# FNet mixing with a GEGLU gate on one core: kept row tiles loaded one unit sooner, rows of g loaded through GpSimd's queue

## The chip, the cores and the metric

The kernel runs on one core of a Trainium2 chip, in float32. The time is that of the device in microseconds (us), the median of several runs. A core has five engines with a queue of instructions each: TensorE (PE, with its weight loads shown apart as PEld), VectorE (DVE), ScalarE (ACT), GpSimd (POOL) and SyncE (SP). SP and POOL also issue DMAs here: SP's are the profile's queue q1, POOL's are q0. All of them run on the core's 16 DMA engines.

## What is computed

x has S = 2048 rows of D = 448, and F = 1792. The reference, cut to what matters:

```python
xn = layernorm(x)
a, b = xn @ dft_hid_re.T, xn @ dft_hid_im.T          # hidden DFT
s = dft_seq_re @ a - dft_seq_im @ b                  # sequence DFT, real part
g = silu((gelu(xn @ w_gate) * (xn @ w_up)) @ w_down) # gate
out = x + s * g
```

## The kernel before, in words

Every matmul operand is split into a high and a low part, and a product is built from two or three matmuls of the parts. The rows are handled in 16 row tiles of 128 (NK = 16).

**The stages.** First the gate g is made (gate and up products, gelu, down product) and collected in SBUF. Then comes the hidden DFT, one row tile k at a time, while g goes through silu (line 930) and is stored row tile by row tile in a DRAM buffer gs (line 931, seen as gv). The hidden DFT leaves, for 14 of the 16 row tiles, an operand TS[k] of seven combinations, split into high and low parts; two row tiles (KP) are kept plain. The last stage, which the change touches, is the sequence DFT with the final product. It begins at about 491 us.

**The last stage.** The output rows are made in eight pairs j of row tiles t. A pair is 16 units u (the loop over `units`, lines 1023 to 1108; m counts units over all pairs). Units 0 to 13 each take one row tile k of TS and do seven products of Strassen's kind into seven PSUM banks (`seven`, lines 975 and 978: a 448-column matmul and a 224-column one for each product, in the order of PRODUCTS). Units 14 and 15 do the two plain row tiles (`plain`). A pair of u = 12 and 13 is done product by product in the last pair (line 1032).

**What is kept and what is reloaded.** Ten of the 14 operands stay in SBUF (KR). The other four (KX: row tiles 4, 5 and 0, 1) share two places, the tiles that the profile calls ts_u: two of them are used in units 0 and 1 of a pair, the other two in units 12 and 13, and the next pair begins with those. All four were saved to DRAM in the stage before (td, line 844, on POOL's queue). So in each pair the two places must be loaded anew between units 0 and 1, which read the old content, and units 12 and 13, which read the new. The load is cut in eight quarters of 392 KB, quarters 0 to 3 for the first place and 4 to 7 for the second (lines 1034 to 1042): quarter i is issued by SP in unit LOAD_AT + i, in the last pair in unit LOAD_AT + i * 7 // 8, which puts its first two in one unit. These loads are the profile's ts_u<-td. A quarter must wait until the matmuls that read what it overwrites are done.

**The left operands.** For each unit the slices of the sequence DFT come from DRAM: ct (192 KB) and sums (128 KB) for units 0 to 13, cp (256 KB) for units 14 and 15 (`load_c`, lines 875 to 882, into buffers that the profile calls raw, f or cc). `sum_c` forms two sums on VectorE (lines 888 and 889), and `prep_c` splits the result: ScalarE copies the high part (line 119), VectorE subtracts for the low part (line 120). `prep_c(m + 3)` is called in unit m, and when it has read its buffer it issues `load_c(m + 8)`. So SP's queue in unit m holds, in this order: the quarter of ts_u if there is one, a load of g if there is one, the loads for unit m + 8, and a store of the output if there is one.

**The end of a pair.** The seven banks are combined by VectorE in units 13 and 14 (`gather`, lines 998 to 1006). In units 0 to 4 of the next pair one step each follows (`give`, lines 1009 to 1019): an addition, in units 1 and 4 the multiplication by g (line 1013) and behind it a DMA on POOL's queue that adds x to the result (line 1015, cc<-x). The stores go out on SP's queue in units 5 and 8 (STORE_AT, line 1017, out<-cc).

**Rows of g.** `load_gx` (line 961) loads the two row tiles of g that pair j needs, 224 KB each, into the ends of two tiles (the profile's ts_g<-gs) in units 11 and 12 (GX_AT). They are read in units 1 and 4 of the next pair, or at the very end (line 1079) in the last one.

The order on each queue is the order of the program; the framework puts in the waits on semaphores that the data need.

Of the kernel before, what the change touches and what calls it, by code (L numbers as in the profile page):

```python
# [45 lines left out]
def fnet_geglu(ctx: ExitStack, tc: tile.TileContext, x, ca, ct, cp, et, wgu, wd, out):  # L46
# [13 lines left out]
    nc = tc.nc  # L60
# [360 lines left out]
    with tc.manual_schedule():  # L421
# [320 lines left out]
        gv = gs.rearrange("p (k d) -> p k d", k=NK)  # L742
# [3 lines left out]
        def place(tag, n):  # L746

            if tag not in new:
                new[tag] = sb.tile([P, n], FR, name=f"ts_{tag}", tag=tag)
            return new[tag]  # L750
# [200 lines left out]
        gx = [place(f"g{t}", 8 * D)[:, T7:].bitcast(F32) for t in range(2)]  # L951
# [6 lines left out]

        def load_gx(j, t):
            if 2 * j + t < NK:  # L960
                nc.sync.dma_start(gx[t], gv[:, 2 * j + t])


        LOAD_AT = 2
        STORE_AT = 5, 8
        GX_AT = 11, 12
        PRODUCTS = {1: (1, 0), 6: (3, 5), 2: (2, 2), 7: (5, 3), 5: (4, 4), 3: (6, 6), 4: (0, 1)}
# [55 lines left out]
        for m, (j, k) in enumerate(units):  # L1023
# [3 lines left out]
            if u < NS:  # L1027
# [7 lines left out]
                for i in range(8):  # L1035
                    if u != LOAD_AT + i * over // 8:
                        continue
# [8 lines left out]
            if u in GX_AT:  # L1046
                load_gx(j, GX_AT.index(u))
# [118 lines left out]
```

## Time and profile before

| | us |
|---|---|
| median of 3 runs | 786.28 (786.23 to 787.33) |
| the profiled execution | 785.82 |
| its span, first to last instruction | 783.9 |
| TensorE busy | 774.9 |
| VectorE busy | 593.7 |
| ScalarE busy | 308.9 |
| GpSimd busy | 51.8 |

The span is what the trace shows; the profiled execution's own time includes what lies around it. A row of a timeline gives the start, the duration, engine, line, operation, what it writes and reads, and in brackets the engine's idle time before it with what ended it. A row of waits gives who waited for what: us in total, times, longest. "To landing" is the time from a DMA's issue to its last byte's semaphore. A stretch view gives the length, the busy time of PE, PEld, DVE, ACT and POOL (with counts), the granted clock of TensorE, the busy share of the 16 DMA engines, and GB/s.

### The profile page before, as it was taken

The page shows a single profiled execution, that of the slowest core. Times are in us where ns is not written, and L with a number is a line of the kernel's source. Part 1 is how long each engine was busy: PE and PEld are TensorE (multiplying, and loading weights), DVE is VectorE, ACT ScalarE, POOL GpSimd, SP SyncE. Part 2 cuts the span into 40 slices and gives each one's busy share as a digit, 9 for nine tenths or more (in the row PEclk, how much of TensorE's full clock was granted, in tenths as well). Part 3 has the DMA queues.
Part 4 walks back from the last instruction along what each step waited for, and adds up shares of the span by engine and source line. Part 5 has one row for each costly group of instructions (what it writes and reads, how often), then busy time and mean ns, then how long its engine had stood idle before and what let it go on. Part 6 is the DMA issues. An engine that isn't in the chain of part 4 may idle for free.

```text
span 783.9 us, 11188 instructions
## 1 busy us (share of the span) xinstructions
PE 774.9 (99%) x4092; PEld 695.4 (89%) x4092; DVE 593.7 (76%) x1045; ACT 308.9 (39%) x430; POOL 51.8 (7%) x82
## 2 busy tenths in 40 slices
PE   9999999999999999999999999999999999999997
PEld 7888888888888888888889999999999999999996
DVE  7877876767766776776675676888888796969686
ACT  3874432331332322322232864544343444444341
POOL 1000211110110010100000000000000000000000
PEclk9999999999999999999999999999999999999999
DMA  8000575353292360546101651778796959697794
GB/s 319 25 3 25 167 220 117 121 121 117 48 258 55 121 135 10 161 131 158 34 13 52 254 229 51 239 256 277 245 318 212 350 172 367 198 322 231 279 278 166
DMA packets 62007, 134.37 MB, mean 171 GB/s; under 512 B 6784, under 2 KB 43520, under 8 KB 61056
## 3 DMA queue, kind: packets, MB, share of 16 engines
q1 hardware_dynamic: 56912, 109.22, 39.7%
q0 software_dynamic: 4896, 24.32, 14.2%
q8 instruction: 32, 0.52, 0.3%
q14 instruction: 23, 0.19, 0.1%
q10 hardware_dynamic: 144, 0.11, 0.0%
HBM read 119.87 MB, written 43.12 MB: 208 GB/s over the span
## 4 chain that ended last, share of the span: by engine, by line
PE 73%; DMA 12%; DVE 10%; issue 2%; SPq 1%; ACT 0%; DVEq 0%
PE x L346 23%; PE po L326 17%; PE ab L803 9%; PE p L975 8%; PE x L354 6%; PE p L978 4%; PE gu L276 4%; DMA ts_u<-td 3%; DMA out<-cc 3%; DVE xt L120 3%; DVE w L120 2%; DMA f<-sums 2%; DMA raw<-sums 2%; DMA raw<-ct 1%; DMA raw<-wgu 1%
## 5 line engine op out<-in xcount | busy, mean ns | idle before, releaser
L326 PE MATMUL po<-wd,hs 128*128 128x448 f32 x672 | 153.0, 366 | 0.0
L326 PEld LDWEIGHTS po<-wd,hs 128*128 128x128 f32 x672 | 125.7, 188 | 14.4
L346 PE MATMUL x<-xt,w 128*128 128x512 f32 x504 | 135.0, 391 | 0.0
L346 PEld LDWEIGHTS x<-xt,w 128*128 128x128 f32 x504 | 94.6, 188 | 16.9
L335 DVE TENSOR_TENSOR gacc<-gacc,po 128x448 f32<-128x448 f32 x96 | 59.1, 618 | 60.9 <-PE po L326 60.9
L119 ACT ACTIVATE w<-raw 128x896 fp32r<-128x896 f32 (+1 forms) x61 | 55.3, 908 | 72.6 <-DVE raw L889 33.7
L346 PE MATMUL x<-thl,w 128*128 128x512 f32 x288 | 77.5, 391 | 0.3 <-DVE tmp L406 0.3
L803 PE MATMUL ab<-w,xt 128*128 128x448 f32 x256 | 68.0, 365 | 0.0
L346 PEld LDWEIGHTS x<-thl,w 128*128 128x128 f32 x288 | 54.0, 188 | 11.6 <-DVE tmp L406 0.7
L354 PE MATMUL x<-xt,w 128*128 128x512 f32 x192 | 59.2, 390 | 0.0
L975 PE MATMUL p<-xt,w 128*128 128x448 f32 x168 | 54.1, 374 | 0.0
L401 ACT ACTIVATE hs<-tmp 128x512 fp32r<-128x512 f32 x24 | 15.2, 634 | 95.3 <-DVE tmp L399 95.3
L803 PEld LDWEIGHTS ab<-w,xt 128*128 128x128 f32 x256 | 48.1, 188 | 3.8
L386 ACT ACTIVATE tmp<-x 128x512 f32<-128x512 f32 x24 | 14.4, 599 | 89.4 <-PE x L354 89.4
L119 ACT ACTIVATE w<-f 128x896 fp32r<-128x896 f32 (+1 forms) x34 | 30.3, 891 | 48.0 <-DVE f L889 26.8
L120 DVE TENSOR_TENSOR w<-raw,w 128x896 fp32r<-128x896 f32 (+1 forms) x41 | 43.0, 1048 | 4.1 <-ACT w L119 3.6
L354 PEld LDWEIGHTS x<-xt,w 128*128 128x128 f32 x192 | 36.0, 188 | 7.7
L975 PE MATMUL p<-ts_u,w 128*128 128x448 f32 x112 | 37.3, 379 | 1.7 <-DMA ts_u<-td 0.7
L975 PE MATMUL p<-ts_u,ts_tmp 128*128 128x448 f32 x112 | 36.5, 374 | 0.0
L888 DVE TENSOR_TENSOR raw<-raw 128x128 f32<-128x128 f32 x69 | 19.9, 288 | 21.2 <-DMA raw<-sums 21.2
L975 PE MATMUL p<-hs,w 128*128 128x448 f32 x112 | 35.6, 374 | 0.0
L803 PE MATMUL ab<-wd,xt 128*128 128x448 f32 x96 | 35.1, 365 | 0.0
(234 smaller groups left out, 1600.0 us busy)
## 6 DMA issues: line engine op xcount, KB each, us to landing
ts_u<-td SPq DMA_DIRECT2D x64, 392.0 KB, 5.9
sums<-ca SPq DMA_DIRECT2D x16, 896.0 KB, 7.5
sums<-ca POOLq DMA_DIRECT2D x16, 896.0 KB, 9.5
raw<-ct SPq DMA_DIRECT2D x69, 192.0 KB, 4.5
raw<-sums SPq DMA_DIRECT2D x69, 128.0 KB, 4.5
f<-ct SPq DMA_DIRECT2D x39, 192.0 KB, 4.4
raw<-wgu SPq DMA_DIRECT2D x14, 512.0 KB, 4.2
td<-ts_u POOLq DMA_DIRECT2D x4, 1568.0 KB, 6.6
```

The lines of the kernel that those rows point to most:

```text
L119: nc.scalar.activation(h, src, AF.Copy)
L120: nc.vector.tensor_sub(l, src, h)
L276: nc.tensor.matmul(ps[:, cols], a, xt[:, k, cols], start=n == 0, stop=n == len(mm) - 1)
L326: nc.tensor.matmul(po[:, :D], hs[:, a, kk * P : (kk + 1) * P], wdn[:, b, i], start=n == 0, stop=n == 5,)
L335: nc.vector.tensor_add(ga, ga, po[:, :D])
L346: nc.tensor.matmul(ps, a[i], b[j], start=first and n == 0, stop=n == 2, skip_group_check=True)
L354: nc.tensor.matmul(ps, w["k3" + "gu"[g]][0], xt[:, 3], start=False, stop=True, skip_group_check=True)
L401: nc.scalar.activation(hs[:, 0], g1, AF.Copy)
L803: nc.tensor.matmul(p[:, :D], a, b, start=n == 0, stop=n == len(mm) - 1)
L888: nc.vector.tensor_add(s2, cr1, s1)
L975: nc.tensor.matmul(ps[q][:, :D], h, v, start=u % UN == 0, stop=False, skip_group_check=True)
L978: nc.tensor.matmul(ps[q][:, :HD], l, v[:, :HD], start=False, stop=u % UN == NS - 1, skip_group_check=True,)
```

## The change

Two edits. LOAD_AT goes from 2 to 1: each quarter of the kept row tiles is issued one unit sooner, in units 1 to 8 in place of 2 to 9 (in the last pair 1 to 7 in place of 2 to 8). And `load_gx` issues its DMA on GpSimd's queue in place of SP's; the place in the program stays (units 11 and 12), but POOL's queue holds nothing else of the stage than the two accumulating DMAs of line 1015.

```diff
         def load_gx(j, t):
             if 2 * j + t < NK:
-                nc.sync.dma_start(gx[t], gv[:, 2 * j + t])
+                nc.gpsimd.dma_start(gx[t], gv[:, 2 * j + t])
...
-        LOAD_AT = 2
+        LOAD_AT = 1
```

## The prediction

> **What bounds the kernel now.** First the page, for which engine sets the time.
>
> ```profile
> span 783.9 us, 11188 instructions
> PE 774.9 (99%) x4092; PEld 695.4 (89%) x4092; DVE 593.7 (76%) x1045; ACT 308.9 (39%) x430; POOL 51.8 (7%) x82
> ```
>
> TensorE is busy 774.9 of 783.9 us (its granted clock is 1.00 in the stretches shown below), and the edit touches none of its work. So the edit can only fill holes between matmuls, or make new ones. The next view is the waits of the weight loads (PEld) from 520 us on, pairs 1 to 7 of the last stage. I take weight loads, not matmuls, because they follow each other with hardly a gap, so that a wait stands there in full.
>
> ```profile
> PEld p L975 <- issue: 1.0, 2, 0.6
> PEld p L975 <- DMA ts_u<-td: 1.0, 2, 0.6
> PEld p L975 <- DMA f<-sums: 0.7, 1, 0.7
> PEld p L975 <- DMA raw<-sums: 0.6, 1, 0.6
> ```
>
> Those are six waits, 1.0 + 1.0 + 0.7 + 0.6 = 3.3 us, all at line 975: **that is all there is to win**. Now the timeline of TensorE around the hole of pair 6, with the start of that pair's unit 1 (708.76) and unit 8 (724.11) ahead of it.
>
> ```profile
> 708.76 0.37 PE L975 MATMUL p<-ts_u,w 128*128 128x448 f32 x1
> ...
> 724.11 0.38 PE L975 MATMUL p<-xt,ts_tmp 128*128 128x448 f32 x1
> ...
> 735.08 0.37 PE L975 MATMUL p<-ts_u,w 128*128 128x448 f32 x1
> 735.29 0.26 PE L978 MATMUL p<-ts_u,w 128*128 128x224 f32 x1
> 736.00 0.44 PE L975 MATMUL p<-ts_u,w 128*128 128x448 f32 x1 [0.45 <-DMA f<-sums]
> ```
>
> Seven units take 724.11 - 708.76 = 15.35 us, 2.19 us each. A matmul of 448 columns holds the stream for 0.21 us (735.08 to 735.29) and one of 224 half as long, so after the one at 735.29 the second product of unit 13 was due at 735.39; it began at 736.00. It reads columns of ts_u that the last two quarters of the second kept tile bring. Which transfer was late is seen in SP's timeline of that pair, and from its issue to landing for the last quarter alone (issued 730.15).
>
> ```profile
> 711.61 0.43 SPq L882 DMA_DIRECT2D f<-sums  x1
> ...
> 714.21 0.38 SPq L1042 DMA_DIRECT2D ts_u<-td  x1
> ...
> 729.35 0.34 SPq L1017 DMA_DIRECT2D out<-cc  x1
> 730.15 0.32 SPq L1042 DMA_DIRECT2D ts_u<-td  x1
> ...
> 734.02 0.32 SPq L961 DMA_DIRECT2D ts_g<-gs  x1
> ```
>
> ```profile
> DMA to landing us min/median/max: 5.7/5.7/5.7
> ```
>
> 730.15 + 5.7 = 735.85, 0.15 us ahead of the delayed matmul. The profile's label names f<-sums, but what the product reads came by the last ts_u quarter; I take it for the releaser of all six holes. Why it lands late shows in the stretch views, from the first quarter's issue to the last one's landing and in a quiet stretch after it (last two numbers: DMA share, GB/s).
>
> ```profile
> 714.21:735.86 21.65, 21.34 (x137) 20.11 (x135) 16.36 (x31) 9.20 (x11) 1.75 (x2) 1.00 1.02 341
> 738.00:750.30 12.30, 12.30 (x74) 11.60 (x73) 12.13 (x24) 4.79 (x5) 0.00 (x0) 1.00 0.46 142
> ```
>
> From the first quarter to the last the DMA engines are full (share 1.02); afterwards they are half idle (0.46). The last quarter lands when the bytes ahead of it have passed, so it is early or late with the start of that stretch and with the bytes in it.
>
> **The change part by part.** *One unit sooner.* The first quarter is now issued in unit 1, ahead of that unit's load of ct and sums. In SP's order that place is just behind the load issued at 711.61, which is over at 711.61 + 0.43 = 712.04. The quarter leaves at about 712.1 in place of 714.21, **2.1 us sooner**. It must wait for unit 0's matmuls, which read the tile that it overwrites; unit 1 began at 708.76, 3.3 us earlier, so this wait is over when SP comes to it and nothing queues behind it. SP's own waits confirm that these issues waited only for landings of earlier DMAs:
>
> ```profile
> SPq L1042 <- DMA ts_u<-td: 7.1, 11, 1.7
> ```
>
> The eight quarters keep their spacing of a unit, and seven loads of ct, sums or cp stand between first and last as before. The bytes between them change in two places only. The store out<-cc of unit 8 is issued at 729.35, ahead of the last quarter at 730.15; when the last quarter belongs to unit 8 the store comes behind it. And the two loads of g move.
>
> *The loads of g.* The 16 DMAs of line 961 (two per pair) leave SP, at 0.32 us of issue each; what SP issues behind them is no wait of TensorE in this trace, so I take that at nothing. On GpSimd's queue they stand behind the accumulating DMA of unit 4 and wait only for the multiplications of units 1 and 4 that read the old g. POOL has nothing else to do then:
>
> ```profile
> 720.41 0.88 POOL L1015 DMA_DIRECT2D cc<-x  x1 [5.32 <-DVE f L888]
> ```
>
> So they leave at about 721.3 and 722.2, not from 734.02 on, and their 2 x 224 KB now pass ahead of the last quarter. They are needed in units 1 and 4 of the next pair, 13 units or 28 us later, so they can't be late themselves. In the last pair the same holds: they come 15 us sooner than today. The price of their bytes has no row of its own, since nothing plain is loaded on POOL's queue in this stage. The bounds come from the queues' shares between 526 and 770 us (packets, MB, share of 16 engines) and from landings in that stretch:
>
> ```profile
> q1 hardware_dynamic: 40577, 62.70, 74.6%
> q0 software_dynamic: 2016, 3.21, 7.7%
> ...
> cc<-x POOLq DMA_DIRECT2D x14, 224.0 KB, 6.2
> out<-cc SPq DMA_DIRECT2D x14, 224.0 KB, 5.7
> ts_g<-gs SPq DMA_DIRECT2D x14, 224.0 KB, 4.2
> ```
>
> q1 (SP): 74.6% of 244 us for 62.70 MB is 2.90 us of all engines per MB. A load of g is 0.229 MB, 0.67 us; two are **1.33 us**. q0 (POOL): 7.7% of 244 us is 18.8 us for 14 accumulates, 1.34 us each, so two at that price are 2.68 us. An accumulate reads, adds and writes back; these loads are plain copies as on SP today, so I take 1.33 and keep 2.68 as the upper end, nothing as the lower.
>
> A rule speaks to where that price falls. The Trainium skill, page "DMA: Bandwidth & Descriptors", section "Queues, rings and completion order", says that each DMA engine serves the queues that have work in turn, packet by packet. By that rule POOL's loads do not wait behind SP's backlog, and the whole price stands ahead of the last quarter, as in the sum below; were POOL's queue served last, the price would be nothing and the landing 1.3 us earlier still. No plain load of this trace decides between the two.
>
> *The sum for the last quarter of pair 6*: 735.85 - 2.1 (start) - 0.67 (store behind it) + 1.33 (g) = 734.4. It is due at 735.39, so the hole goes with 1.0 us to spare; up to a price of about 2.3 us for the g loads it is gone. The last pair differs: its first two quarters leave together, and its store is behind the last quarter already.
>
> ```profile
> 749.48 0.33 SPq L881 DMA_DIRECT2D raw<-ct  x1
> 749.86 0.43 SPq L882 DMA_DIRECT2D raw<-sums  x1
> 750.39 0.85 SPq L1042 DMA_DIRECT2D ts_u<-td  x2
> ...
> 763.71 0.32 SPq L1042 DMA_DIRECT2D ts_u<-td  x1
> ```
>
> ```profile
> 769.97 0.27 PE L978 MATMUL p<-ts_u,xt 128*128 128x224 f32 x1
> 770.60 0.44 PE L975 MATMUL p<-ts_u,w 128*128 128x448 f32 x1 [0.36 <-DMA ts_u<-td]
> ```
>
> The profile releases 770.60 by that quarter. Without the load at 749.48 ahead, it comes about 2.0 us sooner, plus 1.33 for g: 0.7 us sooner in all, where the hole is 770.60 - 770.07 = 0.53 us. It goes with 0.2 us to spare.
>
> *What is late next.* VectorE prepares the left operands about 2.6 us ahead of their use: its low half for unit 8, below, ends at 721.54, and unit 8 began at 724.11.
>
> ```profile
> 720.45 1.09 DVE L120 TENSOR_TENSOR xt<-f,ts_tmp 128x896 fp32r<-128x896 f32 x1
> ```
>
> The g loads delay ct and sums by 1.33 us at most at my price, so this cover holds; if it were gone, each us beyond 2.6 would be a us on TensorE. With the six holes filled, nothing in the stage has TensorE wait. From 3.3 us I take off 0.1 for the gaps that weight loads have anyway: **-3.2 us**. The profiled execution took 785.82 us (783.9 of span, the rest around it untouched), which becomes 782.6. Its own time is 0.46 below the median of the runs, 786.28, for which the forecast is **783.1**.
>
> **The rivals.** *Half of it*: the g price is about 2.4 us. The landing of pair 6 moves by -2.1 - 0.67 + 2.4 = -0.4 us, which fills most of some holes and half of others, and in the last pair by -2.0 + 2.4 = +0.4. Five pairs at about -0.35 and one at +0.4 give -1.35: 784.9. For it speaks POOL's median landing of 6.2 us beside 4.2 for g on SP; against it, that these 6.2 are of accumulates.
>
> *No difference*: the accumulate's price, 2.68. The landing moves by -0.1 us in pairs 2 to 6 and by +0.7 in the last: about 786.4. That is also the time if the earlier issue only queues sooner behind the same bytes; against that stands that the engines have idle share ahead of the stretch.
>
> *Slower*: on POOL's queue each load of g keeps the engines from SP's backlog for the difference of the two landings above, 6.2 - 4.2 = 2.0 us, so 4.0 per pair. It decides from 2.1 + 0.67 = 2.8 us on, where the last quarter lands later than today. Price: 4.0 - 2.77 = 1.2 us in each of pairs 2 to 6 and 4.0 - 2.0 = 2.0 in the last: +8.0, 794.3. For it: the g loads stand exactly in the stretch where the engines are full. Against it: the same bytes on SP's queue cost 0.67 us of engines, and a longer landing is not a longer hold.
>
> A rule against half of the edit: the Trainium skill, page "DMA: Bandwidth & Descriptors", section "Rules for kernel authors", holds that spreading DMAs over several issuing engines brings no bandwidth and saves only issue time. By it the move of g alone is worth nothing here and can only cost, and the -3.2 us must come from the earlier quarters; the trace agrees so far as its engines are full (1.02) with nearly all bytes from one queue.
>
> **How the numbers follow.** Forecast 0.70, half of it 0.12, no difference 0.08, slower 0.10. A difference of 0.2% (1.57 us) is about what a measurement of this kernel can tell from none. The half case, -1.35 with either side of 1.57 possible, is split evenly. Faster: 0.70 + 0.06 = 0.76. Same: 0.06 + 0.08 = 0.14. Slower: 0.10. The range reaches from 782.5 (all 3.3 us and the spread of the runs) over the half case to 786.0; it leaves out the slower case and most of no difference.
>
> **What would show it.** Right: in pairs 1 to 7 no wait of weight loads at line 975 for a DMA; the first ts_u quarter issued about 2 us sooner after its pair's start and the last landing about a us ahead of its product; g's loads on POOL right behind the accumulate of unit 4; a unit still 2.19 us. Wrong: holes that stay in the second product of unit 13 (the price of g was too low), or new waits of TensorE for VectorE's operands in units 8 to 12 (the cover was too thin), or POOL's accumulates landing much later than 6.2 us.

## The result and the profile after

The changed kernel takes **789.13 us** (787.97 to 790.53, six runs) where the one before, run beside it, takes 786.25 (785.77 to 787.33): a ratio of 1.0037, interval 1.0024 to 1.0050. It is slower by 2.9 us. The forecast was 783.1, the range ended at 786.0, and slower had a chance of 0.10. The profiled execution took 788.92 us, 3.1 more than before's 785.82.

The page of the kernel after, its first lines:

```profile
span 786.9 us, 11195 instructions
PE 774.5 (98%) x4092; PEld 695.1 (88%) x4092; DVE 594.3 (76%) x1045; ACT 308.8 (39%) x430; POOL 61.2 (8%) x98
```

TensorE's work is the same (774.5 us), so the 3.0 us of span are holes or tail. The waits of its weight loads from 520 us on (who waited for what, total, times, longest):

```profile
PEld p L975 <- DVE cc L1071: 5.6, 6, 1.2
```

**Every wait for a DMA is gone, as forecast. Six new ones for VectorE stand in their place, 5.6 us where there were 3.3.** TensorE's timeline shows both in pair 6: its unit 1, the start of its unit 13, and the new hole, in unit 0 of pair 7.

```profile
711.55 0.38 PE L975 MATMUL p<-ts_u,w 128*128 128x448 f32 x1
...
737.87 0.38 PE L975 MATMUL p<-ts_u,w 128*128 128x448 f32 x1
738.09 0.26 PE L978 MATMUL p<-ts_u,w 128*128 128x224 f32 x1
738.19 0.38 PE L975 MATMUL p<-ts_u,w 128*128 128x448 f32 x1
...
746.73 0.27 PE L978 MATMUL p<-ts_u,xt 128*128 128x224 f32 x1
747.44 0.47 PE L975 MATMUL p<-ts_u,ts_tmp 128*128 128x448 f32 x1 [0.45 <-DVE cc L1071]
```

The second product of unit 13 follows the first by 0.32 us (737.87 to 738.19); before, it took 0.92. But the product at 747.44 was due at 746.73 + 0.10 = 746.83 and came 0.61 us late. It is the seventh of unit 0, and it writes the PSUM bank that held the plain product of unit 14. Line 1071, the addition on VectorE that takes that product out (it is queued in unit 14 and given in unit 15), had not read the bank yet.

Why line 1071 is late shows in VectorE's timeline of the same kernel, from the end of pair 6 on:

```profile
738.38 0.29 DVE L888 TENSOR_TENSOR raw<-raw 128x128 f32<-128x128 f32 x1 [2.10 <-DMA raw<-sums]
...
738.92 0.68 DVE L120 TENSOR_TENSOR xt<-raw,w 128x512 fp32r<-128x512 f32 x1
739.79 0.29 DVE L888 TENSOR_TENSOR raw<-raw 128x128 f32<-128x128 f32 x1 [0.19 <-DMA raw<-sums]
...
740.33 0.61 DVE L1000 TENSOR_TENSOR cc<-cc,p 128x448 f32<-128x448 f32 x1
...
746.77 0.61 DVE L1071 TENSOR_TENSOR cc<-cc,py 128x448 f32<-128x448 f32 x1
```

VectorE works in program order. Ahead of the gather of pair 6 (line 1000 on) stand the sums (line 888) of units 0 and 1 of pair 7, called in units 12 and 13. At 738.38 VectorE has waited 2.10 us for the DMA that brings them. The gather begins at 740.33, and from there to the end of line 1071 it takes 747.38 - 740.33 = 7.05 us. Now the same steps before the change, which the prediction never looked at:

```profile
734.44 0.29 DVE L888 TENSOR_TENSOR raw<-raw 128x128 f32<-128x128 f32 x1 [2.17 <-DMA raw<-sums]
...
736.73 0.29 DVE L888 TENSOR_TENSOR raw<-raw 128x128 f32<-128x128 f32 x1 [1.07 <-DMA raw<-sums]
...
737.27 0.61 DVE L1000 TENSOR_TENSOR cc<-cc,p 128x448 f32<-128x448 f32 x1
...
743.71 0.61 DVE L1071 TENSOR_TENSOR cc<-cc,py 128x448 f32<-128x448 f32 x1
```

with the seventh product of that unit 0 in before's timeline of TensorE:

```profile
744.69 0.38 PE L975 MATMUL p<-ts_u,ts_tmp 128*128 128x448 f32 x1
```

The chain is as long, 744.32 - 737.27 = 7.05 us, and it ended 0.37 us ahead of the product at 744.69. From this comes a budget. Without holes the seventh product is due 746.83 - 737.87 = 8.96 us after the start of unit 13, so the gather may begin at most 8.96 - 7.05 = **1.91 us** after that start. Before, it began 737.27 - 735.08 = 2.19 us after: 0.28 too late. Nothing showed, because the old hole in unit 13 (0.61) held TensorE back too. After, it begins 740.33 - 737.87 = 2.46 us behind: 0.55 too late, and there is no other hole to cover it. The trace has 0.61.

Last, the queues. SP's timeline of pair 6 after, and the time from issue to landing of the last quarter (issued 730.92) alone:

```profile
715.08 0.38 SPq L1042 DMA_DIRECT2D ts_u<-td  x1
...
730.92 0.32 SPq L1042 DMA_DIRECT2D ts_u<-td  x1
...
732.81 0.42 SPq L882 DMA_DIRECT2D raw<-sums  x1
```

```profile
DMA to landing us min/median/max: 6.5/6.5/6.5
```

The last quarter lands at 737.42, 25.87 us after the pair's unit 1 (711.55); before it was 735.85 - 708.76 = 27.09. The gain is 1.22 us, where the sum had 2.1 + 0.67 - 1.33 = 1.44. And the loads that VectorE waits for, those of the next pair's unit 0, are issued in unit 8: at 732.81, now **behind** the last quarter in SP's order, where they stood ahead of it. GpSimd's timeline shows g:

```profile
723.36 0.88 POOL L1015 DMA_DIRECT2D cc<-x  x1 [5.28 <-DVE f L888]
723.92 1.44 POOL L961 DMA_DIRECT2D ts_g<-gs  x2
```

They leave right behind the accumulating DMA, as forecast, into the stretch where the engines are full.

### The profile page after: what moved, and what is told of

Same layout as the page of the kernel before. It is cut to its first block, busy times and chain, and to the rows that moved or that the text cites. A ratio compares the mean times of both kernels' runs of the same rounds, so it can differ in the third digit from the quotient of the medians.

```text
span 786.9 us, 11195 instructions
## 1 busy us (share of the span) xinstructions
PE 774.5 (98%) x4092; PEld 695.1 (88%) x4092; DVE 594.3 (76%) x1045; ACT 308.8 (39%) x430; POOL 61.2 (8%) x98
## 4 chain that ended last, share of the span: by engine, by line
PE 84%; DVE 7%; DMA 6%; issue 2%; SPq 0%; ACT 0%; DVEq 0%
PE x L346 23%; PE po L326 17%; PE p L975 15%; PE ab L803 9%; PE p L978 7%; PE x L354 5%; PE gu L276 4%; DMA raw<-cp 2%; DVE w L120 2%; DMA ts_u<-td 1%; DMA f<-sums 1%; DVE xt L120 1%; DMA raw<-wgu 1%; PE pt L164 1%; PE py L990 1%
## 5 line engine op out<-in xcount | busy, mean ns | idle before, releaser
L975 PE MATMUL p<-xt,w 128*128 128x448 f32 x168 | 54.1, 374 | 0.0
L975 PE MATMUL p<-ts_u,ts_tmp 128*128 128x448 f32 x112 | 37.5, 380 | 3.9 <-DVE cc L1071 3.9
L975 PE MATMUL p<-ts_u,w 128*128 128x448 f32 x112 | 36.5, 375 | 0.0
L975 PE MATMUL p<-hs,w 128*128 128x448 f32 x112 | 35.6, 374 | 0.0
```

The source lines that it names most:

```text
L975: nc.tensor.matmul(ps[q][:, :D], h, v, start=u % UN == 0, stop=False, skip_group_check=True)
```

## The experiments

Three theories stood against each other. **Late sums**: g's bytes, moved into the full stretch, delay the loads of the next pair's sums, VectorE stands at them, and the gather behind them frees a bank too late. **POOL**: loads on GpSimd's queue are slower or slow the others, whatever the time at which they run. **Moved hole**: once unit 13's hole is filled, VectorE has no time to spare in unit 0, so the hole only moves, whoever fills it.

### One part alone

`sooner_only` keeps the earlier quarters and leaves g on SP.

```diff
-                nc.gpsimd.dma_start(gx[t], gv[:, 2 * j + t])
+                nc.sync.dma_start(gx[t], gv[:, 2 * j + t])
```

> The quarters one unit sooner, g on SP in units 11 and 12 as before. Theory 'late sums' (the new hole in unit 0 comes because VectorE stands in program order at the sums of the next pair's first units, whose loads land later: the last quarter now goes ahead of them on SP's queue, and the bytes of g pass ahead of them too): without g's bytes, 1.0 us a pair, those loads land about 1 us sooner than in the changed kernel, the hole of unit 0 (0.6 to 1.1 us a pair) is nearly gone and the hole of unit 13 too: 783 to 784.5. Rival 'POOL' (a DMA on POOL's queue slows the rest): the same, about 783. Rival 'moved hole' (VectorE's chain at a pair's end had 0.4 us in hand after a hole of 0.3 to 0.7, so filling the hole of unit 13 opens one of about 0.3 us in unit 0 whatever the loads do): 785, with six holes in unit 0.

Measured: 782.68 us (782.33 to 782.97) beside 785.78, ratio 0.9962 (0.9950 to 0.9974). It is 3.1 us faster, nearly what the prediction gave for both edits (3.2). From 520 us on no wait of TensorE is left. Late sums and POOL both expected about this. VectorE's timeline of the pair, then the start of unit 13 and the seventh product in TensorE's:

```profile
731.74 0.29 DVE L888 TENSOR_TENSOR raw<-raw 128x128 f32<-128x128 f32 x1 [1.70 <-DMA raw<-sums]
...
733.04 0.29 DVE L888 TENSOR_TENSOR raw<-raw 128x128 f32<-128x128 f32 x1
...
734.01 0.62 DVE L1000 TENSOR_TENSOR cc<-cc,p 128x448 f32<-128x448 f32 x1 [0.35 <-ACT cc L998]
...
740.46 0.61 DVE L1071 TENSOR_TENSOR cc<-cc,py 128x448 f32<-128x448 f32 x1
```

```profile
706.61 0.37 PE L975 MATMUL p<-ts_u,w 128*128 128x448 f32 x1
...
732.93 0.37 PE L975 MATMUL p<-ts_u,w 128*128 128x448 f32 x1
...
741.86 0.38 PE L975 MATMUL p<-ts_u,ts_tmp 128*128 128x448 f32 x1
```

The gather begins 734.01 - 732.93 = 1.08 us after unit 13's start, inside the 1.91, and line 1071 ends at 741.07, 0.8 us ahead of the product. Moved hole falls in the form "whoever fills it": the hole was filled and none opened. The sums of unit 1 begin 733.04 - 706.61 = 26.43 us after the pair's unit 1; after the whole change it is 739.79 - 711.55 = 28.24, before it 736.73 - 708.76 = 27.97. So the earlier quarters alone bring these sums 1.5 us forward, and g's move takes 1.8 us back.

`pool_only` is the other half.

```diff
-        LOAD_AT = 1
+        LOAD_AT = 2
```

> g on POOL's queue, the quarters at their old place. 'Late sums': g's bytes, 1.0 us of all engines a pair, pass ahead of the last quarter, whose hole in unit 13 grows from 0.3 to 0.7 us to about 1.3 to 1.7; none in unit 0, since the hole of unit 13 gives VectorE its time: 786.25 + 6 x 1.0 + about 1 in pair 1 = 792 to 793. 'POOL' (more than its bytes): above 794. 'Moved hole': as 'late sums', 792.

Measured: 793.47 us (793.11 to 794.90), ratio 1.0105 (1.0090 to 1.0119), so 7.7 us slower than before. Its waits of weight loads are the old ones of unit 13, grown, seven with 11.2 us in place of six with 3.3:

```profile
PEld p L975 <- DMA ts_u<-td: 9.5, 6, 2.0
PEld p L975 <- issue: 1.7, 1, 1.7
```

That is half a us above what late sums expected, and the holes are where it put them. Alone, the move of g is pure cost. The two edits don't add up, though: -3.1 and +7.7 would give +4.6, and the whole change has +2.9, and unit 13 has no hole in it: there the earlier quarters make up for what g takes.

### Is it the queue or the time?

`g_early_on_sp` loads g on SP's queue, in units 5 and 6, about where GpSimd's queue lets it go.

```diff
-                nc.gpsimd.dma_start(gx[t], gv[:, 2 * j + t])
+                nc.sync.dma_start(gx[t], gv[:, 2 * j + t])
...
-        GX_AT = 11, 12
+        GX_AT = 5, 6
```

> The quarters one unit sooner, and the loads of g on SP's queue, but issued in units 5 and 6, about when POOL issues them in the changed kernel. 'Late sums': what counts is that the bytes pass in the full stretch, not whose queue they are on; holes in unit 0 of 0.6 to 1.2 us: 788 to 790. 'POOL': as with g on SP in units 11 and 12, about 783. 'Moved hole': 785.

Measured: 789.03 us (787.73 to 791.48) beside 785.78, ratio 1.0047 (1.0030 to 1.0063). That is the time of the change (789.13), with nearly the same holes, 5.5 us in seven waits where the change has 5.6 in six:

```profile
PEld p L975 <- DVE cc L1071: 4.6, 5, 1.2
PEld p L975 <- issue: 0.9, 2, 0.7
```

In pairs 1 to 6 the first of the two loads leaves 11.9 to 13.7 us after the pair's unit 1 and the second 15.4 to 18.3, where GpSimd sends both at 12.0 to 13.0. So the moments are near, not equal. POOL falls: the same bytes early on SP's queue cost as much. `g_late_on_act` asks the reverse: a queue other than SP's, but late. ScalarE issues g's loads in units 14 and 15.

```diff
-                nc.gpsimd.dma_start(gx[t], gv[:, 2 * j + t])
+                (nc.scalar if j < NK // 2 - 1 else nc.sync).dma_start(gx[t], gv[:, 2 * j + t])
...
-            if u in GX_AT:
-                load_gx(j, GX_AT.index(u))
+            at = GX_AT if j == NK // 2 - 1 else (NS, NS + 1)
+            if u in at:
+                load_gx(j, at.index(u))
```

> The quarters one unit sooner; the loads of g on ScalarE's queue in units 14 and 15, behind the full stretch (in the last pair on SP in units 11 and 12). 'Late sums': the moment decides and not the queue, so as with g on SP in units 11 and 12: 782.3 to 783.3, no hole. A rival by which any second issuing queue costs time: 785 or more.

Measured: 783.10 us (782.24 to 783.97) beside 786.28, ratio 0.9958 (0.9945 to 0.9971); one wait of 0.2 us is left. It is no better than `sooner_only`, so taking g off SP's queue is worth nothing that shows here.

`one_g_early` leaves one of the two loads on GpSimd and puts the other back on SP.

```diff
-                nc.gpsimd.dma_start(gx[t], gv[:, 2 * j + t])
+                (nc.gpsimd, nc.sync)[t].dma_start(gx[t], gv[:, 2 * j + t])
```

> The changed kernel with one load of g of a pair on POOL's queue (so early, in the full stretch) and the other on SP in unit 12. In the runs so far the load of sums for the next pair's unit 1 lands 26.1 to 26.9 us after a pair's unit 1 begins with both loads of g late, and 28.1 to 28.7 with both early, and the hole in unit 0 is what goes beyond about 27.6. 'Late sums': half the bytes, landing at 27.1 to 27.9, holes of 0 to 0.3 us: 782.8 to 784.5. 'POOL': half of the 6.5 us between the two, about 786.

Measured: 784.86 us (783.39 to 785.88), ratio 0.9981 (0.9972 to 0.9989). That lies between the two expectations, and holes of 0 to 0.3 us were expected where the longest is 1.2. Four holes behind VectorE are left, and a small one:

```profile
PEld p L975 <- DVE cc L1071: 2.8, 4, 1.2
PEld p L975 <- issue: 0.2, 1, 0.2
```

Each set against the kernel before that ran beside it, `sooner_only`, this kernel and the change stand at 782.68 - 785.78 = -3.1, 784.86 - 786.28 = -1.4 and 789.13 - 786.25 = +2.9 us. The first half of the bytes cost 1.7 us, the second 4.3. A cost that grows faster than the bytes fits a threshold, like the 1.91 us of the budget, better than a queue that is slow by itself.

### Is it VectorE's wait for the sums?

`gather_first` keeps the change and, in unit 13, puts the first three steps of the gather ahead of the sums.

```diff
-            if m:
+            if m and not (j < NK // 2 - 1 and u in (NS - 2, NS - 1)):
                 sum_c(m + 4)
...
                 todo = gather(ps)
                 for f in todo[:3]:
                     f()
+                sum_c(m + 3)
+                sum_c(m + 4)
                 prep_c(m + 3)
```

> The changed kernel, with VectorE's order at a pair's end turned round: in unit 13 the first three steps of gather come ahead of the sums of the next pair's units 0 and 1. 'Late sums': gather no longer stands behind loads, the bank of py0 is free about 0.7 us sooner, the holes of unit 0 shrink to 0 to 0.4 us each and those of unit 13 stay away: 782.5 to 785. 'POOL': the DMA engines are as slow as before and the operands come late elsewhere: 788 to 790. 'Moved hole': the chain from gather to the bank is as long as before and begins with TensorE's own unit 13, so part stays: 785.

Measured: 790.64 us (790.28 to 791.51), ratio 1.0066 (1.0054 to 1.0078). A miss: it was to win and lost. Its waits, its unit 13 in TensorE's timeline, and VectorE's (line numbers from 1065 on are two higher here, so 1071 is 1073):

```profile
PEld p L975 <- DVE cc L1073: 7.4, 7, 1.1
```

```profile
739.13 0.37 PE L975 MATMUL p<-ts_u,w 128*128 128x448 f32 x1
```

```profile
740.22 0.62 DVE L1000 TENSOR_TENSOR cc<-cc,p 128x448 f32<-128x448 f32 x1 [0.67 <-ACT cc L998]
...
748.35 0.61 DVE L1073 TENSOR_TENSOR cc<-cc,py 128x448 f32<-128x448 f32 x1
```

The gather does begin sooner, 1.09 us after unit 13's start. But the sums of two units are now inside the chain, and behind them 0.54 us of waiting for ScalarE's copy of the high part: from the gather to the end of line 1073 it takes 748.96 - 740.22 = 8.74 us, not 7.05. 1.09 + 8.74 = 9.83 against 8.96 leaves a hole of 0.87. The wait was moved off the sums; their work was moved onto the path. This doesn't say who was right, except that the budget again gives the hole.

`sums_elsewhere` takes the wait away and keeps the work in its place. The sums for units 0 and 1 of the next pairs are formed on a constant tile that is always there (ident): the same instructions, without a wait for a load. The true sums of these left operands are left out.

```diff
                 _, cr1, ci1, s2, s1, _, s4 = [raw_at(m)[:, i * P : (i + 1) * P] for i in range(7)]
+                if m >= UN and m % UN < 2:
+                    cr1 = ci1 = s2 = s1 = s4 = ident
```

> The changed kernel, but the two sums of the units 0 and 1 of a next pair are formed on a tile that is not loaded, so that VectorE does the same work there without waiting for these loads (part of the left operand of those units is left out). The DMAs are those of the changed kernel. 'Late sums': VectorE comes to gather in time, the bank of py0 is free 0.8 us ahead of its use, no hole in unit 0: 782.3 to 783.5. 'POOL', or any theory by which the operands themselves come too late: 788 or more. 'Moved hole': 785.

Measured: 783.58 us (782.76 to 784.49), ratio 0.9966 (0.9954 to 0.9978). No wait of TensorE is left, with g still early on GpSimd's queue. Unit 13 and VectorE there (line numbers from 888 on are two higher):

```profile
733.80 0.37 PE L977 MATMUL p<-ts_u,w 128*128 128x448 f32 x1
```

```profile
733.02 0.28 DVE L890 TENSOR_TENSOR ident<-ident 128x128 f32<-128x128 f32 x1
...
734.88 0.62 DVE L1002 TENSOR_TENSOR cc<-cc,p 128x448 f32<-128x448 f32 x1 [1.25 <-ACT cc L1000]
...
741.34 0.61 DVE L1073 TENSOR_TENSOR cc<-cc,py 128x448 f32<-128x448 f32 x1
```

The gather begins 1.08 us after unit 13 and the chain is 7.07 long. The DMAs stand in the same order on the same queues, and with VectorE's wait for the sums goes the whole loss, 789.13 to 783.58.

One thing moves with it. Without holes the quarters leave sooner, and in pair 6 the load of unit 1's sums lands 27.3 us after the pair's unit 1, where in the change it was 28.15. By the budget a hole opens from about 27.6 on: unit 13 starts 737.87 - 711.55 = 26.32 us after unit 1, the gather may begin 1.91 later, and 0.6 goes for the sums ahead of it. So pair 6 alone would not decide. But in pairs 2, 3 and 5 of this run the load lands at 27.85, 28.48 and 28.75, later than that, and there is no hole there either. **This settles it**: it is VectorE's wait for these loads, and not their lateness as such, that TensorE pays for.

### The order on SP's queue

`last_quarter_in_unit_9` puts only the last quarter back, behind the store and the loads for unit 0 of the next pair.

```diff
-                    if u != LOAD_AT + i * over // 8:
+                    if u != LOAD_AT + i * over // 8 + (i == 7 and j < NK // 2 - 1):
```

> The changed kernel with the eighth quarter issued in unit 9 as before, behind the load for the next pair's unit 0 and ahead of that for unit 1. 'Late sums' in the form that the load for unit 1 lands last and decides: the bytes ahead of that load are the same, no change, 788 to 790. In the form that the load for unit 0 decides (the quarter that was put ahead of it costs 1.1 us): holes nearly gone, 783 to 785.

Measured: 789.75 us (788.35 to 790.38), ratio 1.0039 (1.0027 to 1.0052). The time stays, but the holes go back to unit 13:

```profile
PEld p L975 <- DMA ts_u<-td: 6.8, 6, 2.1
```

The first form had the time right and the place wrong: the last quarter is late again, TensorE waits for it in unit 13, and this wait hides VectorE's, as in `pool_only`. Which of the two loads, that of unit 0 or that of unit 1, decides when the gather begins, this run can't tell. In the trace of the change it is that of unit 1, by little: at 739.79 VectorE waits another 0.19 us for it.

## Why the prediction was wrong

**Step by step.** That 3.3 us were all there was to win was right: `sooner_only` won 3.1. That the first quarter would leave sooner was right: 2.88 us after unit 1 in `sooner_only`, below, where it was 714.21 - 708.76 = 5.45 before, so 2.6 us against a forecast of 2.1. In the change itself it left 715.08 - 711.55 = 3.53 after unit 1, 1.9 us sooner.

```profile
709.49 0.38 SPq L1042 DMA_DIRECT2D ts_u<-td  x1
```

That the holes of unit 13 would go with both edits, by 1.44 us of landing, was right in place and nearly in size (1.22). One reading was wrong without harm: SP's issues at line 1042 waited not only for landings of earlier DMAs, but once, for 0.3 us, for matmuls (SPq L1042 <- PE p L975).

**The price of g** was near. The queues between 526 and 770 us, first after, then in `sooner_only` (packets, MB, share of 16 engines):

```profile
q0 software_dynamic: 2912, 6.42, 10.7%
...
ts_g<-gs POOLq DMA_DIRECT2D x14, 224.0 KB, 7.4
```

```profile
q0 software_dynamic: 2016, 3.21, 7.5%
...
ts_g<-gs SPq DMA_DIRECT2D x14, 224.0 KB, 3.7
```

10.7% less 7.5% of 244 us, 26.1 - 18.3 = 7.8 us, over 14 loads is 0.56 us each and 1.1 per pair, where the prediction took 1.33. The slower rival's price, the difference of landings, is refuted: the landings did lengthen, from 3.7 to 7.4 us, but a longer landing is not a longer hold, as the prediction said there. The time came out on that rival's side by another mechanism, in another unit.

On the rule about the service of queues (the Trainium skill, page "DMA: Bandwidth & Descriptors", section "Queues, rings and completion order": queues with work are served in turn, packet by packet), the runs agree as far as they go: g early on GpSimd's queue cost as much as g early on SP's, 789.13 and 789.03 us, so GpSimd's queue was not served last. That the service goes packet by packet no run shows.

**The step that failed is "*What is late next*"**: "The g loads delay ct and sums by 1.33 us at most at my price, so this cover holds", and "With the six holes filled, nothing in the stage has TensorE wait". The cover was wrong. 2.6 us was read at unit 8, in the middle of a pair, and taken for the stage. At the end of a pair the same loads stand ahead of the gather, and in before's pair 6 the cover there was 0.37 us, of which the old hole itself gave 0.61: without the hole the gather is 0.28 us too late, by the budget above. The earlier quarters bring the sums 1.54 us forward and g's move takes them 1.81 back: -0.28 + 1.54 - 1.81 = -0.55, the new hole. So the cover that g's delay met was 1.26 us in pair 6, and not 2.6.

The delay was also larger than forecast. From `sooner_only` to the change, the sums of unit 1 come 1.7 to 2.0 us later in pairs 1 to 6, against 1.33 at most. Under a cover of 2.6 us that would have cost nothing; under the true one, 0.7 to 1.5 us in these pairs of `sooner_only`, even 1.33 would have opened holes of some 1.4 us in all. That is an estimate from the start of unit 1's sums in each pair: a hole opens where they begin later than 26.32 + 1.91 - 0.54 = 27.69 us after the pair's unit 1. By it the kernel would have taken about 784.5; the rest of the loss is the larger delay and the tail below.

What uses up that cover was in before's rows: VectorE idle for 2.17 and 1.07 us at line 888. TensorE's list of waits could not show it, since TensorE did not wait there yet. Among its signs of being wrong the prediction did name a thin cover on VectorE, but for operands in units 8 to 12, and not for a bank in unit 0.

**The 1.8 us in pair 6** are 1.1 of g's bytes and 0.65 of a later start: the first quarter leaves 715.08 - 711.55 = 3.53 us after unit 1 where it left 2.88 in `sooner_only`. The later start goes with a VectorE that comes late out of the pair before. In the change the first quarter leaves 3.5 to 3.9 us after unit 1 in pairs 2 to 6, each of which begins with a hole behind VectorE, and 2.90 in pair 1, which has none. In `sums_elsewhere`, with g as early and no hole, it leaves after 2.8 to 2.9 in all of them. So a late gather makes the next pair's quarters late too, and with them the sums behind them. Pair 1 has no such later start and shows 1.66 us all the same: some 0.5 us stay open there.

**The sum of the loss.** The waits in the stage went from 3.3 to 5.6 us, +2.3. TensorE's last matmul begins at 781.11 in after's timeline and at 778.78 in before's, 2.33 of the 3.0 us of span. The other 0.7 lies behind the last matmul, where VectorE ends the last pair: its last gather begins at 774.68, before at 771.24, which is 3.4 us later. Why it falls back more than TensorE there stays open.

**The other rule**, that more issuing engines bring no bandwidth (the Trainium skill, the same page, section "Rules for kernel authors"), spoke against half of the edit, and was right: `g_late_on_act` gained nothing over `sooner_only`. The 7.7 us that `pool_only` lost are the price of the moment. The prediction quoted the rule, and then priced the move at the last quarter and at the operands of unit 8 alone.

**What to do.** Of the kernels that compute the whole result, `sooner_only` has the shortest time, 782.68 us: LOAD_AT = 1, g on SP's queue in units 11 and 12. `g_late_on_act` (783.10) can't be told from it.

## What to carry to other kernels

Before a transfer is moved into a stretch where the DMA engines are full, follow every load in that stretch to the engine that waits for it, and that engine's next steps to what they release; the cover is the least over the whole loop, and a hole that is about to be filled may be part of it. Look at the idle times of the engines that do not set the end: a wait of 2 us on VectorE is harmless only as long as the step behind it has time in hand. A DMA that moves to an idle engine's queue moves in time too, so ask for each of them what it would cost early on the old queue.

## What the runs showed of the hardware

A DMA's place in the program did not set its moment. With an idle engine to issue it, g's load called in unit 11 left at 723.92, in the middle of the pair, right behind the accumulating DMA on that queue: 12.4 us after the pair's unit 1, where on SP's it left 734.02 - 708.76 = 25.3 us after it.

A plain load of 224 KB on GpSimd's queue held the engines for 0.56 us (the difference of shares above), less than half of the 1.34 of an accumulating DMA of that size on the same queue. It also takes fewer packets there than on SP's. The queues on the page of after (packets, MB, share):

```profile
q1 hardware_dynamic: 54608, 105.55, 38.5%
q0 software_dynamic: 5920, 27.99, 15.3%
```

Before, q1 had 56912 packets and q0 4896. So the sixteen loads took 2304 packets from q1, 144 each, and came to q0 as 1024, 64 each, for the same 3.67 MB.
